# Sink rows of v: two small DMAs and two wide casts, or 32 small VectorE copies, under a planner with new load rates

## The chip, the cores and the metric

The kernel runs on one core of one Trainium2 chip. The metric is the device time of one execution in microseconds (us), the median of several runs. A hardware profile of one further execution gives the durations.

The engines are called by the names of the profile: PE is TensorE (PEld its weight loads), DVE is VectorE, ACT is ScalarE, POOL is GpSimd and SP is SyncE, which here only issues DMAs.

## The reference

Attention with four sink keys and a sliding window of 128 keys, for 4 batches, 8 heads, 768 positions and 64 values per head, followed by a feed-forward layer with a gated activation over 3072 tokens:

```python
scores = scale * np.matmul(q, k.transpose(0, 1, 3, 2))
keep = is_sink | in_window          # key < 4, or 0 <= query - key < 128
a = softmax(np.where(keep, scores, -1e9))
x = (a @ v) as tokens x 512         # heads side by side
h = x @ w_in                        # 512 -> 2048
out = (h * sigmoid(beta * h)) @ w_out   # 2048 -> 512
```

Inputs and output are float32; the products are made in bf16.

## The kernel before, in words

**Units.** The attention is cut into 32 units n: a batch, a pair of heads and one half (384) of the positions. `place(n)` gives batch `n // 8`, head pair `n % 4`, half `n // 4 % 2` and buffer `n % 4`. Units 0 to 3 are the first halves of the four pairs of batch 0, units 4 to 7 their second halves. A token tile T of 384 tokens needs the four units 4T to 4T+3.

**Steps of a unit.** DMAs load q, k and v in float32 (`load_qk` L425, `load_head` L434). POOL casts them to bf16 (L481 for q and k, L484 for v into the tile `v_aug`, which has a column of ones beside each head's 64 columns, so that the row sums of the softmax come out of the same product). PE transposes q and k (L504), and DVE copies the result from PSUM (`qkT`, L513). PE forms the scores (L560; L552 first adds a mask for the first six units), ACT takes the exponential (L567), PE multiplies with v (`attend`, L647), DVE divides (`normalise`, L656, L658), PE transposes the result (L675) and ACT or DVE copies it into `xT` (L679). From unit 12 on DMA transposes take the place of both PE transposes.

**Sinks.** Second halves (and no first ones) need the four sink keys besides the window. POOL builds `k_sink` (L525), PE forms their scores (L533), ACT the exponentials `E_sink` (L536), and in `attend` one more matmul (L636) multiplies `E_sink` with `v_sink`. `v_sink` holds for each of the 16 pairs of batch and head pair the four first rows of v: head 0 on partitions 0 to 3, head 1 on partitions 32 to 35, in 64 columns each with a column of ones; the rest is zero. Before the change all of it is filled at the start: two DMAs of 16 KB on ACT's queue fetch the float32 rows of every pair into a part of the tile `g` that is free then (L781), and two DVE casts write them into `v_sink` (L800).

**Feed-forward.** For each token tile, `hidden` forms 16 products of 128 features (L695, four matmuls each), ACT takes a tanh (L703), DVE the gate (L717) into `g`, and `project` multiplies with w_out (L744). In the first token tile the hidden products use two PSUM banks in turn, so that a product waits for the gate two before it. The weights come in 16 DMAs of 512 KB through `wst` and are cast by POOL (L469).

**Order.** The program is written as a list of operations with the tiles that they read and write. `Prog.order` plays it through with a cost for each operation and a time at which each engine is free, and picks the next operation of each engine as the one that can start first, among a window of 160 operations. `give` is added to the start of an operation in this comparison, so that one with `give=500` goes behind all that could start within 500 ns. `after` makes an operation wait, in the plan only, until another one is done. What comes out is a fixed order for each engine; at run time each engine goes through its list in order and waits on semaphores for what the tiles demand. So a cost in the plan costs no time itself, but it sets what stands behind what.

For a load the plan has the size divided by a rate in bytes per ns, one load after another over all queues, and a fixed time from the end of the transfer to its landing:

```python
n.done = dma_free[e] + (self.TURNED if n.dma[0][0] in "tx" else
                        self.LANDED if start > 3000.0 else self.FIRST_LANDED)
```

While PE has nothing to do at the start, `keep_busy` puts matmuls on a tile of ones there (L806), which write nothing that is used.

Of the kernel before, what the change touches and what calls it, by code (L numbers as in the profile page):

```python
# [5 lines left out]
F32 = mybir.dt.float32  # L6
# [11 lines left out]
TT = 384  # L18
# [53 lines left out]
class Prog:  # L72
# [12 lines left out]
    AHEAD = {"pe": 160, "act": 160, "dve": 160, "gp": 160, "sp": 40}  # L85
    FIRST_DMA = 0.0
    DEPTH = 7
    LANDED, FIRST_LANDED, TURNED = 2000.0, 1400.0, 4000.0

    def __init__(self):  # L90
        self.nodes = []
# [67 lines left out]
    def order(self):  # L159

        for n in self.nodes:
            n.open = len(n.preds)
            for p in n.preds.values():
                p.succs.append(n)
        free = dict.fromkeys(self.ENGINES, 0.0)
        left = {e: [n for n in self.nodes if n.eng == e] for e in self.ENGINES}
        head = dict.fromkeys(self.ENGINES, 0)
        can = {e: [n for n in left[e] if n.open == 0] for e in self.ENGINES}
        placed = []
        dma_free = dict.fromkeys(self.ENGINES, self.FIRST_DMA)  # L170
        landing = {e: [] for e in self.ENGINES}

        def best(e):
            q = left[e]
            while head[e] < len(q) and q[head[e]].place is not None:
                head[e] += 1
            if head[e] == len(q):
                return None
            last = q[min(head[e] + self.AHEAD[e], len(q) - 1)].id
            c = [n for n in can[e] if n.id <= last]  # L180
            if not c:
                return None
            n = min(c, key=lambda n: (max(n.ready, free[e]) + n.give, n.id))
            start = max(n.ready, free[e])
            if n.dma is not None and len(landing[e]) >= self.DEPTH:
                start = max(start, landing[e][-self.DEPTH])
            return start, n

        while len(placed) < len(self.nodes):
            found = [(*b, e) for e in self.ENGINES if (b := best(e)) is not None]  # L190
            start, n, e = min(found, key=lambda f: (f[0], f[1].id))
            free[e] = start + n.busy
            if n.dma is None:
                n.done = start + n.busy + n.lag
            else:

                begin = max(dma_free[e], start + n.busy)
                others = [o for o in self.ENGINES if o != e and dma_free[o] > begin]
                dma_free[e] = begin + n.lag * (1 + len(others))
                for o in others:  # L200
                    dma_free[o] += min(n.lag, dma_free[o] - begin)
                n.done = dma_free[e] + (self.TURNED if n.dma[0][0] in "tx" else
                                        self.LANDED if start > 3000.0 else self.FIRST_LANDED)
                landing[e].append(n.done)
            n.place = start
            can[e].remove(n)
            placed.append(n)
            for s in n.succs:
                s.open -= 1
                early = s.id in n.soft or s.eng == e and not n.dma  # L210
                s.ready = max(s.ready, start + n.busy if early else n.done)
                if s.open == 0:
                    can[s.eng].append(s)
        return placed
# [64 lines left out]
def bass_streamingllm_window__then__act_swish_beta_kernel(  # L279
# [145 lines left out]
    def load_qk(n, name, queue="sp"):  # L425
        b, hp, half, pb = place(n)
        s = {"q": q, "k": k}[name][b, 2 * hp:2 * hp + 2, half * TT:half * TT + TT, :].rearrange(
            "h (p c) d -> p h (c d)", c=3)
        d = stage[name][pb][:, :, 3 * half:3 * half + 3, :].rearrange("p h c d -> p h (c d)")
        op(queue, lambda e: e.dma_start(d, s),  # L430
           w=[(name + "_stage", pb, half, 0), (name + "_stage", pb, half, 1)],
           dma=f"{name}{pb}_{half}", line=queue == "sp", **transfer(2 * TT * D * 4, 300))

    def load_head(n, name, hh, queue="sp"):  # L434
        b, hp, half, pb = place(n)
        s = {"q": q, "k": k, "v": v}[name][b, 2 * hp + hh, half * TT:half * TT + TT, :].rearrange(
            "(c p) d -> p c d", p=128)
        op(queue, lambda e: e.dma_start(stage[name][pb][:, hh, 3 * half:3 * half + 3, :], s),
           w=[(name + "_stage", pb, half, hh)], dma=f"{name}{pb}_{half}{hh}", line=queue == "sp",
           **transfer(TT * D * 4, 235))  # L440

    def load(n):
        for name in "qkv":
# [18 lines left out]
    def load_w(i):  # L462
        view, src, _ = w_piece(i)
        op("sp", lambda e: e.dma_start(view, src), w=[("wst", i % NW)], dma=f"w{i % NW}",
           line=True, **transfer(1 << 19, 380))

    def cast_w(i):
        view, _, dst = w_piece(i)
# [54 lines left out]
    def sink_keys(n, after=None):  # L523
        pb = place(n)[3]
        op("gp", lambda e: e.tensor_tensor(  # L525
            k_sink[pb][:, 0:2 * HEAD1].rearrange("p (h x) -> p h x", h=2)[:, :, 0:NSINK],
            qkT[pb][:, 0, 1, 0:NSINK].unsqueeze(1).to_broadcast([128, 2, NSINK]), own_head[:, :, :],
            ALU.mult), r=[("qkT", pb, 0), "own_head"], w=[("k_sink", pb)], busy=150.0, lag=100.0,
           after=after)

    def scores_sink(n, bank, name):
        pb = place(n)[3]
# [85 lines left out]
    def attend(n):  # L618
        _, hp, half, pb = place(n)
        z = n % 2  # L620
        where = {}
        for c, tiles in enumerate(CHUNKS[half]):
            at = 0
            for kb, qb, nq in tiles:
                for x in range(nq):
                    where[kb, qb + x] = [(c, hh, at) for hh in range(2)]
                    at += 128
        if n >= XBAR:

            where = {t: [(hh, x // 3, x % 3 * 128) for hh in range(2)]  # L630
                     for x, t in enumerate(BLOCKS[half])}
        with P.together("pe"):
            for mm in range(3):
                m, at = 3 * half + mm, mm * 2 * D1
                if half == 1:
                    op("pe", lambda e, at=at, mm=mm: e.matmul(  # L636
                        av_ps[:, at:at + 2 * D1], E_sink[z][:, mm * 128:mm * 128 + 128],
                        v_sink[:, n // 8 * 4 + hp, :, :].rearrange("p h e -> p (h e)"),
                        start=True, stop=False, skip_group_check=True),
                       r=[("E_sink", z), "v_sink", ("v_sink", 0), ("v_sink", 1)], w=["av"],  # L640
                       **pe(130))
                for hh in range(2):
                    kbs = range(m + 1) if half == 0 else (m - 1, m)
                    for x, kb in enumerate(kbs):
                        c, h2, col = where[kb, m][hh]
                        node = op("pe", lambda e, at=at, hh=hh, kb=kb, c=c, h2=h2, col=col, first=(half == 0 and x == 0),
                           last=(x == len(kbs) - 1): e.matmul(  # L647
                            av_ps[:, at + hh * D1:at + hh * D1 + D1], E[z][:, c, h2, col:col + 128],
                            v_aug[pb][:, kb, hh, :], start=first, stop=last, skip_group_check=True),
                           r=[("E", z, c), ("v_aug", pb, kb // 3)], w=["av"], **pe(65))  # L650
        return node
# [116 lines left out]
    for n in range(2):  # L768
# [3 lines left out]
    load(3)  # L772
    op("act", lambda e: e.dma_start(beta_stage[:, :], moe_beta.rearrange("(m p) -> m p", p=128)),
       w=["beta_stage"], dma="beta")
    wide = [("g", 1, m) for m in range(6)]
    v_rows = g[1][:, 0:6, :].rearrange("p m x -> p (m x)").bitcast(F32)[:, 0:NPAIR * D]
    v_rows = v_rows.rearrange("p (g d) -> p g d", d=D)
    for hh in range(2):
        rows = slice(HEAD1 * hh, HEAD1 * hh + NSINK)
        s = v[:, :, 0:NSINK, :].rearrange("b (g h) s d -> s h (b g) d", h=2)[:, hh]  # L780
        op("act", lambda e, rows=rows, s=s: e.dma_start(v_rows[rows], s), w=[("v_rows", hh)],  # L781
           dma=f"s{hh}", **transfer(1 << 14, 100))
    load_w(0)
    load_w(1)
    load_w(2)
# [9 lines left out]
    cast(0, True)  # L795
    cast(1)
    sink_constants()
    for hh in range(2):
        rows = slice(HEAD1 * hh, HEAD1 * hh + NSINK)
        op("dve", lambda e, hh=hh, rows=rows: e.tensor_copy(v_sink[rows, :, hh, 0:D], v_rows[rows]),  # L800
           r=[("v_rows", hh), "v_sink"], w=[("v_sink", hh), *wide], give=3000.0, **dve(600.0))

    def keep_busy(count, busy, after=None):

        for _ in range(count):
# [42 lines left out]
    transpose_out(3, tr_ps, "tr", "act")  # L848
    for n in range(4):
        sink_keys(n, ended)  # L850


    at = {16: 38, 17: 46, 18: 52, 19: 57, 24: 69, 25: 75, 26: 81, 27: 87}
# [2 lines left out]
    for s in range(-6, S_END + NM):  # L856
# [5 lines left out]
        for n, step in here:  # L862
# [11 lines left out]
            if step == "av":  # L874
# [2 lines left out]
                if n >= XBAR:  # L877
                    later.append(lambda n=n: transpose_out(n))
                if half == 0:
                    later.append(lambda n=n, ended=ended: sink_keys(n, ended))  # L880
            if step == "out":
                if n < XBAR:
                    transpose_out(n)
# [103 lines left out]
```

## Time and profile before

| what | value |
|---|---|
| runs before | 230.42, 229.3, 230.12 us; median 230.12 |
| the profiled execution | 229.11 us |
| its span, first to last instruction | 227.4 us (1.71 us lie outside) |
| granted TensorE clock | 1.0 |
| PE busy | 219.0 us of the span |
| DVE, ACT, POOL busy | 133.9, 139.1, 74.8 us |
| the removed casts L800 | 0.93 and 0.69 us, at 9.44 and 11.95 us |
| the removed DMAs L781 | 16 KB each, issued at 3.47 us by ACT's queue |

A span is cut in stretches below; a start time counts from the first instruction. The busy time of PE is taken from its records, whose ends are modelled because matmuls are pipelined, so a busy PE is not PE at its peak. The chain of waits is followed back from the last instruction: at each step to the work that released it.

### The profile page before, as it was taken

To read this page: it belongs to the slowest core of one execution; us is meant where nothing else is said; L and a number is where in the kernel's file an instruction comes from. 1 tells how busy PE (TensorE), PEld (TensorE's weight loads), DVE (VectorE), ACT (ScalarE), POOL (GpSimd) and SP (SyncE) were. 2 spreads that over 40 slices of the span, in tenths; PEclk is the share of its full clock that TensorE was granted. 3 is DMA by queue.
4 is the path that set the end of the run, shared out by engine and by line. 5 is a ranking of instruction groups with operands and counts; after the bars stand their busy time and mean duration, and the time that the engine had idled before them with its cause. 6 is when DMAs were issued, how large, how long until landed. Compare 5 with 4: busy or idle time off the path is not lost.

```text
span 227.4 us, 4407 instructions
## 1 busy us (share of the span) xinstructions
PE 219.0 (96%) x1716; PEld 121.3 (53%) x1740; DVE 133.9 (59%) x261; ACT 139.1 (61%) x218; POOL 74.8 (33%) x149
## 2 busy tenths in 40 slices
PE   7988998999999999999999999999999999999995
PEld 4554555655455555545555555555555555555454
DVE  5665699699556655535577677565656555353300
ACT  2666896694437667535976766856676764555410
POOL 7776856699344321544202342500000000000000
PEclk9999999999999999999999999999999999999999
DMA  6999999995679999998999897621101101111022
GB/s 188 318 362 291 331 326 262 393 328 134 139 174 220 303 172 224 242 220 162 250 260 197 192 225 195 153 72 63 52 16 63 63 20 63 46 49 46 13 79 92
DMA packets 95436, 39.78 MB, mean 175 GB/s; under 512 B 81960, under 2 KB 88376, under 8 KB 95416
## 3 DMA queue, kind: packets, MB, share of 16 engines
q1 hardware_dynamic: 93760, 38.75, 66.2%
q10 hardware_dynamic: 1656, 0.76, 1.2%
q8 instruction: 13, 0.21, 0.4%
q14 instruction: 7, 0.06, 0.1%
HBM read 27.30 MB, written 6.29 MB: 148 GB/s over the span
## 4 chain that ended last, share of the span: by engine, by line
PE 90%; DVE 5%; ACT 3%; issue 1%; DVEq 0%
PE acc L744 33%; PE h_ps L695 30%; PE s_ps L647 5%; PE acc L695 4%; PE s_ps L597 4%; PE s_ps L560 2%; ACT E L567 2%; DVE g L717 2%; PE h_ps L744 2%; PE s_ps L504 1%; PE acc L806 1%; DVE E L578 1%; PE h_ps L552 1%; PE s_ps L533 1%; PE s_ps L636 1%
## 5 line engine op out<-in xcount | busy, mean ns | idle before, releaser
L744 PE MATMUL acc<-w_out,g 128*128 128x512 bf16 x328 | 89.3, 380 | 1.3 <-issue 0.5
L703 ACT ACTIVATE th<-h_ps,beta_half 128x384 f32<-128x384 f32 x104 | 59.6, 582 | 45.4 <-PE h_ps L695 43.8
L695 PE MATMUL h_ps<-xT,w_in 128*128 128x384 bf16 x416 | 81.0, 326 | 0.2
L717 DVE SCALAR_TENSOR_TENSOR g<-th,h_ps 128x384 bf16<-128x384 f32 x104 | 56.7, 552 | 38.9 <-ACT th L703 37.6
L695 PEld LDWEIGHTS h_ps<-xT,w_in 128*128 128x128 bf16 x416 | 39.9, 98 | 32.1 <-DVE g L717 1.4
L744 PEld LDWEIGHTS acc<-w_out,g 128*128 128x128 bf16 x352 | 32.0, 98 | 29.7 <-issue 3.5
L613 DVE TENSOR_TENSOR E<-E,mask_all 128x1536 bf16<-128x1536 bf16 x20 | 19.2, 958 | 20.2 <-ACT E L604 20.2
L604 ACT ACTIVATE E<-s_ps 128x1536 bf16<-128x1536 f32 x20 | 28.9, 1445 | 2.0 <-PE s_ps L597 1.9
L481 POOL CAST qk<-q_stage 128x384 bf16<-128x384 f32 x32 | 18.5, 578 | 21.5 <-DMA q_stage<-in_q_dram 14.3
L484 POOL CAST v_aug<-v_stage 128x384 bf16<-128x384 f32 x32 | 17.2, 548 | 23.1 <-DMA v_stage<-in_v_dram 13.0
L481 POOL CAST qk<-k_stage 128x384 bf16<-128x384 f32 x31 | 16.4, 527 | 16.5 <-DMA k_stage<-in_k_dram 15.8
L647 PEld LDWEIGHTS s_ps<-v_aug,E 128*128 128x128 bf16 x384 | 17.3, 97 | 5.5 <-ACT E L567 0.5
L752 ACT ACTIVATE out_sb<-acc 128x512 f32<-128x512 f32 x22 | 13.0, 596 | 11.6 <-PE acc L744 10.9
L695 PE MATMUL acc<-xT,w_in 128*128 128x384 bf16 x96 | 19.1, 327 | 0.9 <-DVE g L717 0.7
L647 PE MATMUL s_ps<-v_aug,E 128*128 128x65 bf16 x384 | 19.5, 193 | 0.4 <-DVE E L578 0.2
L658 DVE TENSOR_TENSOR o_norm<-s_ps,rden 128x384 bf16<-128x384 f32 x32 | 17.8, 557 | 1.5
L567 ACT ACTIVATE E<-s_ps 128x768 bf16<-128x768 f32 x16 | 12.9, 808 | 9.1 <-PE s_ps L560 9.1
L703 ACT ACTIVATE th<-acc,beta_half 128x384 f32<-128x384 f32 x24 | 13.9, 581 | 5.9 <-PE acc L695 5.5
L717 DVE SCALAR_TENSOR_TENSOR g<-th,acc 128x384 bf16<-128x384 f32 x24 | 12.9, 549 | 6.0 <-ACT th L703 5.9
L695 PEld LDWEIGHTS acc<-xT,w_in 128*128 128x128 bf16 x96 | 8.5, 98 | 6.5 <-DVE g L717 1.4
L469 POOL CAST w_in<-wst 128x1024 bf16<-128x1024 f32 x8 | 8.4, 1050 | 6.3 <-DMA wst<-in_moe_w_in_dram 6.2
L597 PE MATMUL s_ps<-qkT 64*128 64x256 bf16 (+2 forms) x144 | 10.1, 254 | 0.0
(75 smaller groups left out, 157.7 us busy)
## 6 DMA issues: line engine op xcount, KB each, us to landing
out_dram<-out_sb SPq DMA_DIRECT2D x23, 256.0 KB, 2.6
wst<-in_moe_w_in_dram SPq DMA_DIRECT2D x8, 512.0 KB, 5.6
wst<-in_moe_w_out_dram SPq DMA_DIRECT2D x8, 512.0 KB, 10.2
q_stage<-in_q_dram SPq DMA_DIRECT2D x8, 384.0 KB, 4.3
k_stage<-in_k_dram SPq DMA_DIRECT2D x8, 384.0 KB, 4.3
v_stage<-in_v_dram SPq DMA_DIRECT2D x8, 384.0 KB, 3.8
v_stage<-in_v_dram SPq DMA_DIRECT2D x30, 96.0 KB, 4.3
q_stage<-in_q_dram SPq DMA_DIRECT2D x12, 192.0 KB, 4.7
```

The lines of the kernel that those rows point to most:

```text
L481: op(eng, lambda e, x=x, name=name: e.tensor_copy(qk16[z][:, x, :, :, :], view(name)), r=[(name + "_stage", pb, half, hh) for hh in range( ...
L484: op("gp", lambda e: e.tensor_copy(v_aug[pb][:, 3 * half:3 * half + 3, :, 0:D], view("v")), r=[("v_stage", pb, half, hh) for hh in range(2 ...
L567: op("act", lambda e: e.activation(E[n % 2][:, c, :, 0:at], bank[:, 0:2, 0:at], AF.Exp, bias=0.0, scale=SCALE), x=[f"{name}0", f"{name}1"] ...
L597: op("pe", lambda e, kb=kb, bank=bank, qb=qb, at=at, nq=nq, rows=rows: e.matmul(s_ps[:, bank, 128 * at:128 * (at + nq)], qkT[pb][rows, kb ...
L604: op("act", lambda e: e.activation(E[z][:, :, :, :].rearrange("p c h x -> p c (h x)"), s_ps[:, :, :].rearrange("p (h b) x -> p h (b x)", h ...
L613: op("dve", lambda e: e.tensor_tensor(both, both, mask_all[:, half, :].unsqueeze(1).to_broadcast([128, 2, 768]), ALU.mult), r=[("E", z, 0) ...
L647: last=(x == len(kbs) - 1): e.matmul(av_ps[:, at + hh * D1:at + hh * D1 + D1], E[z][:, c, h2, col:col + 128], v_aug[pb][:, kb, hh, :], sta ...
L658: op("dve", lambda e: e.tensor_tensor(o_norm[o][:, :, :, :].rearrange("p m h d -> p (m h) d"), src[:, :, 0:D], rden[z][:, :].unsqueeze(2). ...
L695: return op("pe", lambda e: e.matmul(bank, w_in16[:, c, m * 128:(m + 1) * 128], xT[:, c, T * TT:(T + 1) * TT], start=(c == 0), stop=(c == 3)),
L703: op("act", lambda e: e.activation(th[i % 3][:, :], bank, AF.Tanh, bias=0.0, scale=beta_half[:, m:m + 1]), x=[name], r=["beta"], w=[("th", ...
L717: op("dve", lambda e: e.scalar_tensor_tensor(g[T % 2][:, m, :], th[i % 3][:, :], 1.0, bank, ALU.add, ALU.mult), r=[("th", i % 3)], x=[name ...
L744: node = op("pe", lambda e: e.matmul(bank, g[T % 2][:, m, t * 128:(t + 1) * 128], w_out16[:, m, :], start=(m == 0), stop=(m == NM - 1)), r ...
```

## The change

The two DMAs and the two casts go. In their place, `sink_rows(n)` copies the four first rows of v for the pair of unit n out of the bf16 tile `v_aug` on DVE, two copies of 4 x 64 for each of the 16 first halves. It is called beside `sink_keys`, after `attend(n)` (for units 0 to 3 after `attend(3)`). `attend` of a second half now depends on the two copies of its own pair in place of the two casts.

Four of the planner's numbers change: loads of q and k from 300 to 360 bytes per ns, loads of one head from 235 to 285, weights from 380 to 390, and the shorter landing of 1400 ns for loads that start in the first 3 us is dropped, so that all land after 2000 ns.

```diff
--- before.py
+++ after.py
@@ -85,7 +85,7 @@
     AHEAD = {"pe": 160, "act": 160, "dve": 160, "gp": 160, "sp": 40}
     FIRST_DMA = 0.0
     DEPTH = 7
-    LANDED, FIRST_LANDED, TURNED = 2000.0, 1400.0, 4000.0
+    LANDED, TURNED = 2000.0, 4000.0
 
     def __init__(self):
         self.nodes = []
@@ -199,8 +199,7 @@
                 dma_free[e] = begin + n.lag * (1 + len(others))
                 for o in others:
                     dma_free[o] += min(n.lag, dma_free[o] - begin)
-                n.done = dma_free[e] + (self.TURNED if n.dma[0][0] in "tx" else
-                                        self.LANDED if start > 3000.0 else self.FIRST_LANDED)
+                n.done = dma_free[e] + (self.TURNED if n.dma[0][0] in "tx" else self.LANDED)
                 landing[e].append(n.done)
             n.place = start
             can[e].remove(n)
@@ -429,7 +428,7 @@
         d = stage[name][pb][:, :, 3 * half:3 * half + 3, :].rearrange("p h c d -> p h (c d)")
         op(queue, lambda e: e.dma_start(d, s),
            w=[(name + "_stage", pb, half, 0), (name + "_stage", pb, half, 1)],
-           dma=f"{name}{pb}_{half}", line=queue == "sp", **transfer(2 * TT * D * 4, 300))
+           dma=f"{name}{pb}_{half}", line=queue == "sp", **transfer(2 * TT * D * 4, 360))
 
     def load_head(n, name, hh, queue="sp"):
         b, hp, half, pb = place(n)
@@ -437,7 +436,7 @@
             "(c p) d -> p c d", p=128)
         op(queue, lambda e: e.dma_start(stage[name][pb][:, hh, 3 * half:3 * half + 3, :], s),
            w=[(name + "_stage", pb, half, hh)], dma=f"{name}{pb}_{half}{hh}", line=queue == "sp",
-           **transfer(TT * D * 4, 235))
+           **transfer(TT * D * 4, 285))
 
     def load(n):
         for name in "qkv":
@@ -462,7 +461,7 @@
     def load_w(i):
         view, src, _ = w_piece(i)
         op("sp", lambda e: e.dma_start(view, src), w=[("wst", i % NW)], dma=f"w{i % NW}",
-           line=True, **transfer(1 << 19, 380))
+           line=True, **transfer(1 << 19, 390))
 
     def cast_w(i):
         view, _, dst = w_piece(i)
@@ -527,6 +526,16 @@
             qkT[pb][:, 0, 1, 0:NSINK].unsqueeze(1).to_broadcast([128, 2, NSINK]), own_head[:, :, :],
             ALU.mult), r=[("qkT", pb, 0), "own_head"], w=[("k_sink", pb)], busy=150.0, lag=100.0,
            after=after)
+
+    def sink_rows(n, after=None):
+        _, hp, _, pb = place(n)
+        pair = n // 8 * 4 + hp
+        for hh in range(2):
+            rows = slice(HEAD1 * hh, HEAD1 * hh + NSINK)
+            op("dve", lambda e, hh=hh, rows=rows: e.tensor_copy(
+                v_sink[rows, pair, hh, 0:D], v_aug[pb][0:NSINK, 0, hh, 0:D]),
+               r=[("v_aug", pb, 0), "v_sink"], w=[("v_sink", pair, hh)], busy=100.0, lag=140.0,
+               after=after, give=500.0)
 
     def scores_sink(n, bank, name):
         pb = place(n)[3]
@@ -637,7 +646,8 @@
                         av_ps[:, at:at + 2 * D1], E_sink[z][:, mm * 128:mm * 128 + 128],
                         v_sink[:, n // 8 * 4 + hp, :, :].rearrange("p h e -> p (h e)"),
                         start=True, stop=False, skip_group_check=True),
-                       r=[("E_sink", z), "v_sink", ("v_sink", 0), ("v_sink", 1)], w=["av"],
+                       r=[("E_sink", z), "v_sink", *(("v_sink", n // 8 * 4 + hp, hh) for hh in range(2))],
+                       w=["av"],
                        **pe(130))
                 for hh in range(2):
                     kbs = range(m + 1) if half == 0 else (m - 1, m)
@@ -772,14 +782,6 @@
     load(3)
     op("act", lambda e: e.dma_start(beta_stage[:, :], moe_beta.rearrange("(m p) -> m p", p=128)),
        w=["beta_stage"], dma="beta")
-    wide = [("g", 1, m) for m in range(6)]
-    v_rows = g[1][:, 0:6, :].rearrange("p m x -> p (m x)").bitcast(F32)[:, 0:NPAIR * D]
-    v_rows = v_rows.rearrange("p (g d) -> p g d", d=D)
-    for hh in range(2):
-        rows = slice(HEAD1 * hh, HEAD1 * hh + NSINK)
-        s = v[:, :, 0:NSINK, :].rearrange("b (g h) s d -> s h (b g) d", h=2)[:, hh]
-        op("act", lambda e, rows=rows, s=s: e.dma_start(v_rows[rows], s), w=[("v_rows", hh)],
-           dma=f"s{hh}", **transfer(1 << 14, 100))
     load_w(0)
     load_w(1)
     load_w(2)
@@ -795,11 +797,6 @@
     cast(0, True)
     cast(1)
     sink_constants()
-    for hh in range(2):
-        rows = slice(HEAD1 * hh, HEAD1 * hh + NSINK)
-        op("dve", lambda e, hh=hh, rows=rows: e.tensor_copy(v_sink[rows, :, hh, 0:D], v_rows[rows]),
-           r=[("v_rows", hh), "v_sink"], w=[("v_sink", hh), *wide], give=3000.0, **dve(600.0))
-
     def keep_busy(count, busy, after=None):
 
         for _ in range(count):
@@ -848,6 +845,7 @@
     transpose_out(3, tr_ps, "tr", "act")
     for n in range(4):
         sink_keys(n, ended)
+        sink_rows(n, ended)
 
 
     at = {16: 38, 17: 46, 18: 52, 19: 57, 24: 69, 25: 75, 26: 81, 27: 87}
@@ -877,7 +875,7 @@
                 if n >= XBAR:
                     later.append(lambda n=n: transpose_out(n))
                 if half == 0:
-                    later.append(lambda n=n, ended=ended: sink_keys(n, ended))
+                    later.append(lambda n=n, ended=ended: (sink_keys(n, ended), sink_rows(n, ended)))
             if step == "out":
                 if n < XBAR:
                     transpose_out(n)
```

## The prediction

> **What bounds the kernel now.** I read the page's span and busy shares first, then its chain of waits, then a table by stage, and last the order of time between 8 and 20 us. The page:
>
> ```profile
> span 227.4 us, 4407 instructions
> ...
> PE 219.0 (96%) x1716; PEld 121.3 (53%) x1740; DVE 133.9 (59%) x261; ACT 139.1 (61%) x218; POOL 74.8 (33%) x149
> ...
> PE 90%; DVE 5%; ACT 3%; issue 1%; DVEq 0%
> ```
>
> TensorE (PE) is busy for 219.0 of 227.4 us and is 90% of the chain; no DMA and no GpSimd (POOL) stands in it. So an edit can save only time in which PE waits, or runs fillers (the L806 matmuls on ones). The table by stage says where that is; its columns are stretch, length, then busy us of PE, PEld, VectorE (DVE), ScalarE (ACT) and POOL, granted clock, DMA share, GB/s:
>
> ```profile
> 8.00:11.64 3.64, 3.64 (x51) 2.15 (x48) 3.24 (x7) 1.71 (x3) 3.08 (x6) 1.00 1.07 318
> 11.64:16.34 4.70, 4.37 (x57) 2.81 (x54) 2.85 (x6) 3.77 (x6) 3.43 (x7) 1.00 1.03 366
> 16.34:20.54 4.20, 3.64 (x28) 1.98 (x27) 1.86 (x4) 2.12 (x4) 3.13 (x7) 1.00 1.05 282
> 20.54:29.20 8.66, 8.31 (x84) 4.72 (x81) 6.04 (x10) 7.27 (x12) 5.89 (x11) 1.00 1.05 334
> 29.20:37.40 8.20, 7.21 (x94) 4.46 (x91) 8.11 (x18) 6.80 (x11) 6.66 (x10) 1.00 1.03 299
> 37.40:54.00 16.60, 15.92 (x121) 9.24 (x123) 14.33 (x31) 12.84 (x23) 12.60 (x19) 1.00 0.87 296
> ```
>
> PE idles 0 + 0.33 + 0.56 + 0.35 + 0.99 + 0.68 = 2.91 us here; 54 to 200 us lose about 1.3 us more, scattered. Ten fillers between 8 and 20 us, 0.11 us each in the chain, add 1.1 us. From 29.20 to 37.40 DVE is busy 8.11 of 8.20 us: an instruction put there lengthens the run. DMA is saturated (share about 1.05) from 5 to 37 us. Everything this change can do on a large scale lies before 54 us.
>
> The rows around the removed work (start, us, engine, line; in brackets the idle time before and its releaser):
>
> ```profile
> 9.44 0.93 DVE L800 CAST v_sink<-g 4x1024 bf16<-4x1024 f32 x1
> ...
> 9.77 0.96 POOL L481 CAST qk<-q_stage 128x384 bf16<-128x384 f32 x1
> ...
> 10.29 0.93 DVE L513 COPY qkT<-s_ps 128x768 bf16<-128x768 bf16 x1
> ...
> 11.95 0.69 DVE L800 CAST v_sink<-g 4x1024 bf16<-4x1024 f32 x1
> ...
> 12.65 0.96 DVE L513 COPY qkT<-acc 128x768 bf16<-128x768 bf16 x1
> ...
> 17.75 1.04 POOL L469 CAST w_in<-wst 128x1024 bf16<-128x1024 f32 x1 [1.07 <-DMA wst<-in_moe_w_in_dram]
> ...
> 19.11 0.56 DVE L717 SCALAR_TENSOR_TENSOR g<-th,acc 128x384 bf16<-128x384 f32 x1 [1.96 <-ACT th L703]
> ```
>
> Both casts stand directly in front of a qkT copy, and a POOL cast beside the first takes 0.96 us where its like take 0.51; DVE is empty for 1.96 us before 19.11.
>
> **The change part by part.** (1) The two casts go: 0.93 + 0.69 = 1.62 us of DVE. On the path they cost little: the transposes (L504) end at 10.11 and 12.50, the copies start at 10.29 and 12.65, so 0.18 + 0.15 = 0.33 us at most, and PE has far-mask matmuls to run meanwhile, so 0 at least. The POOL cast beside the first cast gets back 0.96 - 0.51 = 0.45 us, which brings n=3's q and k forward.
>
> The Trainium skill (SBUF — State Buffer, Who interferes with whom) says that a VectorE copy or cast that uses both SBUF ports and a GpSimd instruction exclude each other for the whole instruction; the 0.96 us row agrees. By that rule the eight new early copies could hold a POOL cast up by their own length in turn, and the sum would be up to 0.8 us worse if POOL were on the path then.
>
> (2) The two DMAs of 16 KB go. Their issue (0.87 us on ACT's queue at 3.47) hides nothing: ACT's next work is at 5.60. Their transfer does matter. By the issue rows q of n=2 lands at 2.87 + 4.7 = 7.57 and k at 3.40 + 5.2 = 8.60, 1.03 us apart; the like pair of n=3 lands at 4.99 + 4.7 = 9.69 and 5.52 + 4.6 = 10.12, 0.43 us apart. So up to 0.6 us of a saturated queue is theirs; by bytes alone, 32 KB at the 320 GB/s of that stretch, 0.1 us. I take 0.5, since the gap is measured where they run. All later loads then land about that much sooner, w_in piece 3 (17.75) among them, and behind it on POOL the q and k casts of n=4 (18.73, 19.19).
>
> (3) 32 copies of 4x64 come. No row has one; below lies the 4x16 memset (0.072 us), above the 128x6 reciprocal from PSUM (0.192 us). I take 0.1 us, nearest the memset, as both lie in SBUF in four partitions: 3.2 us of DVE (2.3 to 6.1). Eight (n = 0 to 3) become ready with the end of attend(3), as sink_keys do, give way to anything due within 0.5 us, and fit into the 1.96 us gap before 19.11 with 0.8 us (0.6 to 1.5): nothing on the path. If that cover is missed they fall where DVE has no gap, and cost those 0.8 us. The first reader, attend(4), runs at 25.51 (L636), so no wait arises there. The other 24 lie behind attends 8 to 11, 16 to 19 and 24 to 27, where DVE is 49 to 87% busy by the stretches and the next reader is 16 or more steps away: nothing; without that cover 2.4 us. Nobody waits anew for the v_aug tile: POOL's next cast into it already waits for attend(n+4), which itself needs the copies.
>
> The Trainium skill (VectorE: DVE Perf Modes, The TRN2 errata) speaks against this part: many small SBUF copies each pay a fixed cost, 58 cycles plus elements, which I estimate as (58 + 16) / 0.96 GHz = 0.08 us. By it the sum stays as it is, since no copy is on the path.
>
> (4) The planner's costs. They decide the order of every queue, and here the trace can be held against them. Before, the first load is due at 0.81 + 0.525 + 0.655 + 1.4 = 3.39 us; POOL's cast of it starts at 4.08. With the new numbers: 0.81 + 0.525 + 0.546 + 2.0 = 3.88, close to the trace. The loads up to n=3 were planned late: k of n=3 at 0.81 + 0.525 + 8x0.655 + 6x0.418 + 0.33 + 0.1 + 2.0 = 11.5 against a landing at 10.1; now, 0.81 + 0.525 + 8x0.546 + 6x0.345 + 0.1 + 2.0 = 9.9. So PE's queue has n=3's transposes (11.72, 12.17) and scores (13.93) later than the data asks. ACT idles 0.81, 1.14 and 0.76 us before the exponentials of n=1, 2, 3 (9.00, 11.66, 14.31).
>
> **The sum**, against the profiled execution's own 229.11 us (span 227.4 and 1.71 outside), which is 1.0 below the median 230.12. From 8 to 16.34 us PE can win 0.33 idle and 6 fillers of 0.11, together 1.0; I take 0.7, as PE is otherwise dense. From 16.34 to 20.54 the earlier w_in piece and n=4's casts give 0.4 of the 0.5 above (0 to 0.6). From 20.54 to 37.40, 1.34 us idle, I take 0.4 (0 to 1.3): transposes of n=5 run at 22.30 though its k cast ends at 21.06. Copies 0. Together -1.5 us: 227.6 by the profiled run, 228.6 by the median. Its bounds: at least 1.2, the smallest gain that still counts as faster (0.7 of the first stretch and 0.5 of the DMAs'), and at most 1.0 + 0.6 + 1.3 = 2.9 with 0.4 of the scattered 1.3 us behind 54 us, 3.3: 226.8 to 228.9.
>
> **The rivals.** *Slower: the planner runs ahead of the DMA.* In the old plan w_in piece 3 is due at 0.81 + 0.525 + 8x0.655 + 8x0.418 + 0.33 + 0.1 + 4x1.380 + 2.0 = 17.9, and the trace has 17.75: over a long stretch the old rates are right. The new rates fit single transfers but not the sum: 0.81 + 0.525 + 8x0.546 + 8x0.345 + 0.1 + 4x1.344 + 2.0 = 15.9, while the chip can hardly land it before 17.75 - 0.6 = 17.15. n=4's q and k lie behind it. If their transposes move ahead of hidden(0) and hidden(1) in PE's queue, PE stands for them and the tanh-gate chain of the first token tile, which sets 16.3 to 40 us, starts late. Price: 15.9 to 17.2, 1.3 us for w_in and about as much again where n=6 and 7 lie behind two more weight pieces, less half of the 1.1 us won before: +1.3 to +2, so 231.6. It decides once PE waits more than 1 us in all for POOL before L504. For it: PE is in order, and one such wait shows already (0.36 us at 19.30). Against it: one stall shifts PE for all later arrivals, and in the old order L504 mostly came after its data. 23 in 100.
>
> *Slower: the copies miss the gap* and fall into 29.20 to 37.40: +0.8 to +1.5 for eight, and some of the later ones; 231.4. It decides if the planner sees under 1.3 us of gap. The trace's gap is 1.96. 5 in 100.
>
> *No change:* the removed work was covered (DVE and DMA are not in the chain), the exponentials stay where they are because PE was dense from 8 to 11.64, and what is won before 20 us is lost in the DVE-bound stretch. That gives -0.2 to -0.8 us, 229.7. For it: the path cost of each removed piece alone is under 0.6 us. 22 in 100.
>
> **How the numbers follow.** The forecast has the other 50 in 100. About 0.5% (1.15 us) is what a measurement of this kernel can tell from no change: faster is under 228.97, slower over 231.27. Faster 0.50, within 0.22, slower 0.28. The forecast's own range is 226.8 to 228.9; the range of all reaches over both slower cases' prices, down a little for the scattered 1.3 us: 226.5 to 231.7.
>
> **What would show it.** Right: no DMA g<-in_v_dram; k of n=2 lands near 8.1; the POOL cast of n=3's q back at 0.51; eight copies of about 0.1 us between 16 and 19 us; the exponentials of n=3 before 14.0; 29 to 37 us unchanged in DVE's load; PE idle before 54 us near 2. Wrong: PEld L504 waiting for POOL for over 1 us around 17 to 20 us; copies between 29 and 37 us; the last matmul after 225 us in spite of an earlier attend(3).

## The result

The changed kernel takes 232.13 us in the median (231.62 to 233.19, 5 runs) against 230.12 us before. The ratio is 1.0113, interval 1.0086 to 1.0140: slower by 1.1%, where 0.7% faster was forecast. The profiled execution took 232.9 us (span 231.2, mean granted clock 0.992). Its page:

```profile
span 231.2 us, 4461 instructions
...
PE 221.5 (96%) x1740; PEld 121.5 (53%) x1740; DVE 139.7 (60%) x291; ACT 139.7 (60%) x218; POOL 74.4 (32%) x149
...
PE 88%; DVE 8%; ACT 2%; issue 0%; DVEq 0%
```

DVE has come into the chain: 8% of the span in place of 5%. The same stretches as before (the edit shifts the line numbers: L512 here is L513 of before; columns: length, busy us of PE, PEld, DVE, ACT and POOL, granted clock, DMA share, GB/s):

```profile
8.00:11.64 3.64, 3.64 (x51) 2.25 (x51) 2.29 (x6) 2.12 (x4) 2.50 (x6) 1.00 1.09 336
11.64:16.34 4.70, 4.59 (x62) 2.93 (x58) 2.45 (x6) 3.88 (x6) 3.47 (x6) 1.00 1.05 381
16.34:20.54 4.20, 2.32 (x18) 1.10 (x17) 4.08 (x10) 1.64 (x3) 3.54 (x9) 1.00 1.07 276
20.54:29.20 8.66, 7.72 (x65) 3.83 (x66) 5.12 (x9) 5.11 (x9) 6.09 (x11) 0.80 1.08 340
29.20:37.40 8.20, 7.49 (x95) 4.68 (x93) 7.68 (x18) 7.28 (x12) 6.56 (x11) 1.00 1.00 278
37.40:54.00 16.60, 14.87 (x116) 8.79 (x113) 14.09 (x29) 11.11 (x20) 13.53 (x22) 1.00 0.96 312
```

Up to 16.34 us the change wins a little. Between 16.34 and 20.54 PE idles 1.88 us in place of 0.56, while DVE is full: 4.08 of 4.20 us, in place of 1.86. From 20.54 to 29.20 PE's granted clock is 0.80 in the mean. The order of time there (start, us, engine, line) shows what fills DVE:

```profile
16.83 3.62 DVE L535 COPY v_sink<-v_aug 4x64 bf16<-4x64 bf16 x8
...
17.12 1.04 POOL L468 CAST w_in<-wst 128x1024 bf16<-128x1024 f32 x1 [0.66 <-DMA wst<-in_moe_w_in_dram]
...
18.10 0.51 POOL L480 CAST qk<-q_stage 128x384 bf16<-128x384 f32 x1
...
18.55 0.51 POOL L480 CAST qk<-k_stage 128x384 bf16<-128x384 f32 x1
...
20.46 0.96 DVE L512 COPY qkT<-s_ps 128x768 bf16<-128x768 bf16 x1
...
21.34 1.01 DVE L727 SCALAR_TENSOR_TENSOR g<-th,acc 128x384 bf16<-128x384 f32 x2
...
21.48 0.34 PE L542 MATMUL h_ps<-qkT,k_sink 128*128 128x384 bf16 x1 [2.02 <-DVE qkT L512]
```

The eight early copies take 3.62 us. Behind them wait the qkT copy of n=4, whose transposes were done a microsecond earlier, and the first two gates (19.11 before, 21.34 now); PE stands for 2.02 us. The chain of waits gives the copies one by one (start, length, engine, tile, line):

```profile
17.00 0.18 DVE v_sink L535
...
17.20 1.00 DVE v_sink L535
...
18.21 0.44 DVE v_sink L535
...
18.66 0.43 DVE v_sink L535
```

The first two take 0.16 to 0.18 us. The one at 17.20 finds POOL's w_in cast running (17.12 to 18.16) and ends at 18.19. The next begins at 18.21, inside POOL's q cast (18.10 to 18.61), and ends at 18.65; the next ends with the k cast, and so on: one copy for each POOL cast, six of the eight held up, each ending 0.03 to 0.04 us after a cast.

### The profile page after: what moved, and what is told of

The parts are those of the page before. It is cut to its first block, busy times and chain, and to the rows that moved or that the text cites. A ratio compares the mean times of both kernels' runs of the same rounds, so it can differ in the third digit from the quotient of the medians.

```text
span 231.2 us, 4461 instructions
## 1 busy us (share of the span) xinstructions
PE 221.5 (96%) x1740; PEld 121.5 (53%) x1740; DVE 139.7 (60%) x291; ACT 139.7 (60%) x218; POOL 74.4 (32%) x149
## 4 chain that ended last, share of the span: by engine, by line
PE 88%; DVE 8%; ACT 2%; issue 0%; DVEq 0%
PE acc L754 34%; PE h_ps L705 29%; PE s_ps L657 5%; PE acc L705 4%; PE s_ps L606 4%; DVE g L727 2%; DVE qkT L512 2%; PE h_ps L754 2%; PE s_ps L569 2%; DVE v_sink L535 1%; ACT E L576 1%; DVE E L587 1%; PE acc L803 1%; PE h_ps L561 1%; PE s_ps L503 1%; PE s_ps L561 1%
## 5 line engine op out<-in xcount | busy, mean ns | idle before, releaser
L754 PE MATMUL acc<-w_out,g 128*128 128x512 bf16 x352 | 96.6, 380 | 0.0
L705 PE MATMUL h_ps<-xT,w_in 128*128 128x384 bf16 x416 | 81.9, 326 | 0.0
L622 DVE TENSOR_TENSOR E<-E,mask_all 128x1536 bf16<-128x1536 bf16 x20 | 19.9, 995 | 20.4 <-ACT E L613 20.4
L512 DVE COPY qkT<-s_ps 128x768 bf16<-128x768 bf16 (+1 forms) x10 | 9.2, 916 | 2.5 <-PE s_ps L503 2.4
```

The costliest lines, as they stand in the source:

```text
L512: op(eng, lambda e: (e.copy if eng == "act" else e.tensor_copy)(dst, src), x=[tag], w=w, **(act(n * TT) if eng == "act" else dve(65.0 + n ...
L622: op("dve", lambda e: e.tensor_tensor(both, both, mask_all[:, half, :].unsqueeze(1).to_broadcast([128, 2, 768]), ALU.mult), r=[("E", z, 0) ...
L705: return op("pe", lambda e: e.matmul(bank, w_in16[:, c, m * 128:(m + 1) * 128], xT[:, c, T * TT:(T + 1) * TT], start=(c == 0), stop=(c == 3)),
L754: node = op("pe", lambda e: e.matmul(bank, g[T % 2][:, m, t * 128:(t + 1) * 128], w_out16[:, m, :], start=(m == 0), stop=(m == NM - 1)), r ...
```

## The experiments

Two theories were put against each other. **L** (lock): the slow part is the copies standing behind POOL's casts. **R**: the slow part is the planner's new numbers, which run ahead of the DMA (the prediction's first rival). A third, **H**, came up after the first four runs: what counts is how many hidden products of the first token tile stand in PE's queue ahead of the attends of n = 4 to 7. Ratios are against the kernel before, run beside each on the same chip, with 95% intervals.

| run | what it is | ratio | interval |
|---|---|---|---|
| e1_rates_only | before, four new load numbers | 1.0065 | 1.0037 to 1.0093 |
| e2_copies_only | changed, old load numbers | 1.0041 | 1.0024 to 1.0057 |
| e3_reduce | changed, tensor_reduce for each copy | 1.0070 | 1.0043 to 1.0097 |
| e4_act | changed, copies on ACT | 1.0081 | 1.0055 to 1.0108 |
| e5_reduce_old | e2 with tensor_reduce | 1.0023 | 0.9998 to 1.0048 |
| e6_w290 | e1 with weights at 290 | 1.0022 | 1.0006 to 1.0038 |
| e7_landing_only | before, first landing 2000 | 1.0043 | 1.0026 to 1.0060 |
| e8_reduce_w290 | e3 with weights at 290 | 1.0022 | 1.0008 to 1.0037 |
| e9_reduce_win290 | e3 with w_in alone at 290 | 1.0002 | 0.9984 to 1.0019 |
| e10_copy_win290 | changed, w_in alone at 290 | 1.0056 | 1.0030 to 1.0082 |
| e11_reduce_old_win290 | e5 with w_in at 290 | 1.0070 | 1.0047 to 1.0093 |
| e12_rates_win290 | e1 with w_in alone at 290 | 0.9984 | 0.9967 to 1.0000 |

### The two halves apart: e1 and e2

e1 takes the diff's four numbers alone, e2 everything but these numbers.

> The kernel before with the planner's four new load numbers alone; the two DMAs and the two casts stay. Theory L (the new copies stand behind POOL's casts, one each): no copy is in it, so within 0.7 us of the kernel before, ratio 0.997 to 1.003, and no stretch around 17 to 21 us in which PE waits for DVE. Theory R (the planner now runs ahead of the DMA, my rival): 1.3 to 2 us slower than before, ratio 1.006 to 1.009, with PE's L504 waiting over 1 us in all for POOL.

> The changed kernel with the old load numbers and the short first landing: the copies without the new rates. Theory L: the eight early copies again take about 3.5 us in place of 0.8 to 1.4, most of them 0.4 us or more, each ending where a POOL cast ends; 1.5 to 2.6 us slower than before (ratio 1.006 to 1.011), about like the changed kernel. Theory R: at or below the kernel before (ratio 0.993 to 1.000).

Each half is slower by itself: 0.65% and 0.41%, which together make 1.06 of the 1.13%. e1 lies in theory R's range; e2 lies above R's and below L's. Each half has an order of its own as well, so it is no proof that the sum comes out. In e2 three of the eight copies ended with a POOL cast (0.97, 0.43, 0.44 us), fewer than expected, since there the w_in cast started 0.6 us later. In e1 PE waits for POOL before the transposes of n=4, now both ahead of the third hidden product in its queue (weight loads; in brackets the idle time and its releaser):

```profile
19.08 0.17 PEld L503 LDWEIGHTS s_ps<-ident,qk 128*128 128x128 bf16 x3 [0.86 <-POOL qk L480]
19.53 0.17 PEld L503 LDWEIGHTS s_ps<-ident,qk 128*128 128x128 bf16 x3 [0.28 <-POOL qk L480]
```

All such waits between 12 and 54 us come to 1.5 us in e1 and to 0.4 before. The larger loss is behind them: the third tanh still begins with before's (20.57 beside 20.58 us), the fourth 1.22 us later. With the loads planned earlier, the attends of n = 4 to 7 come earlier in PE's queue and push hidden products of the first token tile back. Counted in the queues, 6, 9, 11 and 13 products stand ahead of these four attends before, 5, 7, 9 and 11 in e1, and 4, 6, 8 and 10 in the changed kernel. The products left over then run alone, two banks in turn, at the pace of tanh and gate, 1.30 us apart: the tanh of product 14 (counted from 0) starts at 41.16 us in place of 38.98. This is read from one trace; no run changes the order alone.

### Is it the port, or the smallness of the copies? e3 and e4

```diff
-            op("dve", lambda e, hh=hh, rows=rows: e.tensor_copy(
-                v_sink[rows, pair, hh, 0:D], v_aug[pb][0:NSINK, 0, hh, 0:D]),
+            op("dve", lambda e, hh=hh, rows=rows: e.tensor_reduce(
+                v_sink[rows, pair, hh, 0:D], v_aug[pb][0:NSINK, 0, hh, 0:D].unsqueeze(2),
+                axis=mybir.AxisListType.X, op=ALU.max),
```

> The changed kernel with each of the 32 copies written as a VectorE tensor_reduce (maximum over an axis of one element), same data, same planner costs, so the same order on every engine. Theory L with the Trainium skill's rule (a copy takes both SBUF ports of VectorE and excludes GpSimd, a tensor_reduce never does): every one takes 0.25 us or less also beside POOL casts, the eight of 16.8 us are through by 18.6 and not 20.5, qkT of n=4 starts at or before 19.6; 1.2 to 2.6 us faster than the changed kernel, 229.5 to 231. If the copies are slow for another reason (small SBUF operands, the change of partitions from 0 to 32, semaphores): as slow as the copies, 232.

The instructions of the line in the changed kernel and in e3 (ns: least, median, most):

```profile
L535 DVE COPY v_sink<-v_aug x32: 158/176/997, 16.8 to 167.4; 4x64 bf16<-4x64 bf16 x32
```

```profile
L535 DVE TENSOR_REDUCE v_sink<-v_aug x32: 196/210/214, 16.8 to 166.9; 4x64 bf16<-4x64 bf16 x32
```

A reduce is 34 ns slower in the middle and never waits, though four of the eight early ones ran beside POOL's w_in cast. They were through at 18.56 us. The Trainium skill says so (SBUF — State Buffer, Who interferes with whom): a tensor_reduce never contends with GpSimd, a copy in a two-port mode and a GpSimd instruction shut each other out; these runs agree. That it is a port is the page's word; the runs show that the form of the instruction decides. The gain was smaller than expected: 1.0113 to 1.0070, with intervals that overlap, and qkT of n=4 began at 20.03 and not by 19.6, because PE's queue was still the changed kernel's: here PE waited 2.2 us for POOL before its transposes (12 to 54 us; 0.9 in the changed kernel), which the copies' stall had covered in part.

e4 has `op("act", ... e.copy(...), busy=200.0, ...)` in place of the DVE copies.

> The changed kernel with the 32 copies on ACT (planned at 200 ns each, so the order is planned anew). Theory L: ACT has no port in common with POOL; each copy 0.15 to 0.3 us whatever POOL does, no copy ends with a POOL cast; total 229 to 231, 1 to 3 us faster than the changed kernel. Theory R: the stalls come from the load numbers, which are in it unchanged: about 232.

Every ACT copy took 0.226 to 0.248 us whatever POOL did, as theory L says. The total, 1.0081, hardly moved from 1.0113: as theory R expected, and outside what L alone had given.

### Old numbers without the lock: e5

> The copies-only kernel (old load numbers) with tensor_reduce in place of each copy; the same order on every engine as with the copies. Theory L (lock alone makes copies-only slower): back at the kernel before, ratio 0.997 to 1.001. Theory H (what counts is how many hidden products of the first token tile stand in PE's queue ahead of the attends of n = 4 to 7; before 6, 9, 11, 13, here 5, 8, 10, 12, some 0.6 us for each product missing): most of the 0.9 us stays, ratio 1.001 to 1.004, and the three blocked copies were worth 0.4 us at most.

1.0023 against e2's 1.0041, same order on every engine. The value lies in theory H's range and outside L's, but its interval reaches into both, so it decides between neither. Nothing is left that the new rates or the copies' waits could cost, and still the kernel is not faster than before: the removal of the DMAs and the casts shows no gain, in an order that is not before's (5, 8, 10 and 12 products).

### Which of the numbers: e6, e7, e8

The diff's weights at 390 bytes per ns plan w_in piece 3 at 15.9 us. e6 and e8 plan it near the 17.75 of the trace of before:

```diff
-           line=True, **transfer(1 << 19, 390))
+           line=True, **transfer(1 << 19, 290))
```

> The kernel before with the new numbers for q, k, v and landing, but weights at 290 bytes per ns in place of 390, so that w_in piece 3 is planned at 17.8 us as the trace has it (four pieces at 1.81 us in place of 1.34). Theory H: hidden products ahead of the attends 4 to 7 are 7, 10, 12, 14, one more than before; 0 to 1 us faster than before, ratio 0.996 to 1.000, against 1.0065 with 390. If the planner's early load numbers are harmful in themselves (early landing, q, k, v): still 1.004 or more.

> The kernel before with the landing of the first loads at 2000 ns alone; all rates old. Its plan is later, not earlier, than the old one, so planned ahead of the DMA (rival R) it is not: R says no change, ratio 0.998 to 1.001. Theory H: products ahead of the attends are 6, 8, 10, 12, one fewer for three of the four, so 0.3 to 0.8 us slower, ratio 1.001 to 1.0035.

> The changed kernel with tensor_reduce for the copies and weights at 290 in the plan: no DMAs for the sinks, no wide casts, no lock, w_in planned where the trace has it. Theory H: products ahead of the attends are 6, 9, 11, 13 as before, so within 0.5 us of before, 229.0 to 230.2 beside 229.8 (ratio 0.997 to 1.002), 1.7 to 2.5 us faster than the changed kernel. If the removal of the DMAs itself or the 32 small instructions cost time later in the run: 1.004 or more.

With 290, e6 recovers 0.43 of e1's 0.65%, and e8 0.48 of e3's 0.70%. Both had caught up with before by the tanh at 81 us (81.31 and 81.38 beside 81.32 us) and lost 0.8 and 0.9 us between there and 183 us, so both ratios missed the expected values by a little. e7 misses the ranges of both theories: 1.0043. Its loss lies ahead of what they were asked about: the first tanh starts at 19.56 in place of 18.49 us, against 18.48 in e1, where the other numbers stand beside the later landing. The exponentials of n=0 already begin 0.47 us late (7.15 beside 6.68), and the rest comes at n=3, by the same waiting as in the changed kernel, here of an old wide cast that began inside a POOL cast:

```profile
12.39 1.04 POOL L469 CAST w_in<-wst 128x1024 bf16<-128x1024 f32 x1 [0.94 <-DMA wst<-in_moe_w_in_dram]
...
12.47 1.50 DVE L800 CAST v_sink<-g 4x1024 bf16<-4x1024 f32 x1
...
15.00 0.34 PE L560 MATMUL s_ps<-qkT 64*128 64x384 bf16 x2 [0.81 <-DVE qkT L513]
```

In the kernel before this cast took 0.69 us.

### A clean pair: e9 and e10, and e12 beside them

```diff
-           line=True, **transfer(1 << 19, 390))
+           line=True, **transfer(1 << 19, 290 if i < NW else 390))
```

> As the reduce kernel with weights at 290, but only the eight w_in pieces planned at 290; the w_out pieces are planned at 390 as in the changed kernel. Products ahead of the attends 6, 9, 11, 13. The kernel with all at 290 had caught up with before by 81 us and lost 0.8 us between there and 170 us. If that came of w_out's planned rate: 229.0 to 229.8 beside 229.6, ratio 0.997 to 1.001. If it is the ordinary scatter of a new plan: unchanged, 1.001 to 1.004.

> The same with VectorE copies in place of tensor_reduce, every engine in the same order: the changed kernel with only w_in's planned rate altered. Theory L: several of the eight early copies again end with a POOL cast at 0.4 us and more; 0.4 to 1.2 us slower than its reduce twin (ratio against before 0.002 to 0.005 higher). Theory R and H: about 1.3 to 2 us faster than the changed kernel (1.0113), so 1.002 to 1.006, as w_in is no longer planned ahead of the trace.

> The kernel before (DMAs and wide casts kept) with the new load numbers but w_in at 290: 390 for w_out. Products 7, 10, 12, 14. If w_in's rate alone made the rates-only kernel slower (1.0065): 0.998 to 1.002. If the early landing and the q, k, v rates carry it: 1.004 or more.

e9 and e10 differ in the 32 instructions alone; the order on every engine is the same. DVE in e9:

```profile
16.26 1.76 DVE L535 TENSOR_REDUCE v_sink<-v_aug 4x64 bf16<-4x64 bf16 x8
18.30 1.03 DVE L728 SCALAR_TENSOR_TENSOR g<-th,acc 128x384 bf16<-128x384 f32 x2 [0.28 <-ACT th L714]
```

and in e10:

```profile
17.00 3.31 DVE L535 COPY v_sink<-v_aug 4x64 bf16<-4x64 bf16 x8
20.32 1.02 DVE L727 SCALAR_TENSOR_TENSOR g<-th,acc 128x384 bf16<-128x384 f32 x2
```

The first two gates start 2.02 us later, and the third hidden product waits for the first gate's bank: its tanh is at 22.43 us in place of 19.77. In e10 five of the eight early copies take 0.43 to 0.95 us, each begun while a POOL cast was running, and five of the 24 later ones take 0.35 to 0.48 us in the same way. In time the lock makes 1.0056 of 1.0002, 0.54%, and the intervals lie apart. About half of it comes through the clock (last section). From the changed kernel (1.0113) to e10, w_in's planned rate makes 0.57%, with intervals that all but touch; from e1 to e12 it makes 0.81%. e9 came back to before, as expected if w_out's rate made the rest in e8 (1.0022), but those two intervals overlap. e12, with the DMAs and wide casts kept, has the lowest ratio of all: 229.24 us beside 229.75, 0.9984, whose interval reaches 1.0000, so no more than a hint of a gain.

### Later still: e11

> tensor_reduce copies, all old load numbers except w_in at 290, so the plan is later than the trace by some 1.4 us at w_in piece 3 and more behind it. Products ahead of the attends 7, 10, 12, 14, one more than before. Theory H: at or below before, ratio 0.995 to 1.000. If an order that is too late costs as much as one too early: 1.002 to 1.006.

1.0070: a miss. More hidden products ahead of the attends are therefore no rule for the whole time. The early part came out as the count says, the tanh of product 20 at 44.09 beside 44.55 us, and 81.62 beside 81.32 us at product 40. Then 1.7 us were lost between 81 and 183 us. Why a new plan wins or loses up to that much in the later attends (e6, e8 and e11 lost there, e1 won 0.5) stays open.

## Why the prediction was wrong, point by point

**The removed casts.** Their POOL neighbour came back to 0.51 us (q of n=3, at 8.98), as predicted. Casts and DMAs together won 0.24 us on the path up to n=3 (below), so the casts were as little on it as they were said to be.

**The removed DMAs.** k of n=2 lands at 3.4 + 4.3 = 7.7 us, 0.9 sooner than the 8.6 of before and sooner than the predicted 8.1. Over all traces it lands at 7.70 to 8.40 in the nine kernels without the DMAs (median 7.94) and at 8.30 to 8.64 in the five with them (8.44), so the 0.5 taken was right there. POOL's cast of w_in piece 3 (17.12) and n=4's q cast (18.10) start 0.63 us sooner in the changed kernel, but e3, with the same order, has this w_in cast at 17.65, and e2 and e9, also without the DMAs, have it at 17.71 and 17.63, beside 17.75 before: that all later loads land sooner, the source of 0.4 us of the sum, is not borne out. Nor was what the DMAs delayed the bound: the last exponentials of n=3 begin at 14.78 us (15.02 before), the reciprocal of n=3 at 16.12 (16.36). So 0.24 us was won up to there where 0.7 was taken; from 8 to 16.34 us PE idles 0.33 us before and 0.11 now, so there was little to win. (The fillers between 8 and 20 us are nine, not ten, which changes no term of the sum.) Of the forecast gain of 1.5 us, e9, which has neither the lock nor w_in's early rate, keeps nothing: 1.0002.

**The copies: the step that failed.** Alone a copy takes 0.158 to 0.178 us, inside the bounds of 0.072 and 0.192, above the 0.1 taken and twice the estimate of 0.08. The error was to price it by rows in which POOL plays no part, and to let the 1.96 us gap cover it. POOL casts without a break from 17.12 to 20.4 us, and in the gap of before it already stood there (17.75). The row that showed the exclusion, a POOL cast of 0.96 us beside a DVE cast, was read one way only: as what the copies might do to POOL. The other way stood in the rows of before as well: the first wide cast (0.93 us, from 9.44) began inside this POOL cast, the second, beside none until its last 0.1 us, took 0.69:

```profile
9.32 0.51 POOL L484 CAST v_aug<-v_stage 128x384 bf16<-128x384 f32 x1
```

Turned round it was what POOL does to the copies: six waits for casts of 0.5 to 1.0 us instead of eight times 0.1. The term was 3.6 us and not 0.8, and the gap hid under 2 us of it. The 24 later copies were nothing here, as said: 0.16 to 0.22 us each.

**The planner's numbers: right as a rival, underweighted.** The prediction wrote down that the new rates fit single transfers and not their sum, priced that at 1.3 to 2 us and gave it 23 in 100. e1 measured 1.5 us (0.65% of 230). Its point of decision, over 1 us of PE waiting for POOL before the transposes, came true in e1 (1.5 us); in the changed kernel it shows 0.9 us only, because the copies held the same chain already (2.2 us in e3, without their waits). That w_in's rate is the number that costs is shown by e1 and e12. Not foreseen was how it costs: by the trace of e1 less by PE standing at the transposes than by hidden products that are moved back behind the attends. This last step is argued; the count of products did not hold as a rule for the whole time (e6, e7, e11). What was taken for the gain, earlier transposes for n=4 and 5, is the same movement seen from the other side: qkT of n=4 to 7 in e1 did start 0.8 to 1.2 us sooner, and the run was longer.

**The range.** The planner's rival was on the list and happened. The copies' rival was there too, but as another mechanism: copies that miss the gap and fall into 29 to 37 us. They did fall into the gap, from 16.83 us, and outgrew it. The list had one slower case at a time, and here two came together: 232.13 lies 0.4 above the upper end.

## What to carry to other kernels

Before small VectorE copies or casts are put into a gap, look at what GpSimd does in it: a copy that begins inside a GpSimd cast lasted here until the cast's end, and a form that was never held up (here a tensor_reduce over one element) cost its own 0.2 us. A planner's load rates have to fit when the last of a row of loads lands, not the distance between two: 390 plans 1.34 us for a piece, and the first three w_in casts of the changed kernel do start 1.36 and 1.33 us apart, but the fourth starts 2.17 us later, 1.2 us behind the 15.9 of the plan. When an edit changes a planner's costs as well, run the two halves apart before explaining the sum.

## What was not expected of the hardware

Behind PE's wait of 2.02 us, which ended at 21.48, the granted clock fell. In the profiled execution of the changed kernel it was 0.50 for 3.41 us, and in that of e10, behind a wait of 2.38 us, just as long (columns as in the table by stage); before it was 1.00 in every stretch of that table:

```profile
20.54:22.72 2.18, 1.24 (x14) 0.79 (x15) 1.96 (x4) 0.87 (x2) 0.93 (x3) 1.00 1.02 363
22.72:26.13 3.41, 3.41 (x17) 1.06 (x16) 1.36 (x2) 2.05 (x4) 3.17 (x6) 0.50 1.17 340
26.13:29.20 3.07, 3.07 (x38) 1.98 (x37) 1.80 (x4) 2.19 (x5) 1.99 (x4) 1.00 1.02 325
```

```profile
20.84:24.25 3.41, 3.32 (x15) 1.78 (x15) 1.68 (x4) 0.58 (x1) 1.55 (x2) 0.50 0.99 336
```

The Trainium skill (TensorE: Matmul & The Clock Gate, The HAM clock gate) has the clock at half rate after an idle window of about 3.4 us that runs freely. The half rate agrees; but here waits of 2.02 and 2.38 us were enough, and not always. Of five runs of the changed kernel, two had a mean clock of 0.992 and 0.993 and took 232.9 and 233.19 us, and three had 1.0 and took 231.62 to 232.13. Of e10's eleven runs, six had 0.985 to 0.993 and took 231.08 to 232.65 us, and five had 1.0 and took 230.05 to 231.05. So the dip is worth about 1.2 us when it comes, on top of the wait. e9 never had it (0.999 or more in twelve runs): with the full clock the lock costs 0.7 us (median of e10's five runs 230.30, of e9 229.62), with all runs 1.46. The only other runs with the dip are five of e4's nine and one of e3's seven, where PE also waits over 2 us around 19 to 21 us, in two pieces. Why such waits bring it in some runs only is not shown; a window that runs freely would fit.
